# A gated recurrence and a two-layer MLP on one core: weights as float32 through the input queue, cast on three engines

## The chip, the cores and the metric

The kernel runs on one core of a Trainium2 chip. TensorE (PE) multiplies matrices, VectorE (DVE), ScalarE (ACT) and GpSimd (POOL) do elementwise work, SyncE (SP) issues transfers, and 16 DMA engines carry them. The metric is the device time of one execution in microseconds. Four runs of the kernel before gave a median of 192.86 us (191.88 to 193.99).

## The reference

For each of 4 batches and 8 heads of width 48, a state of 48 x 48 is carried over 768 steps; then an MLP runs over all 3072 tokens.

```python
f = 1.0 / (1.0 + np.exp(-f_logit))
for t in range(S):
    state = f[:, :, t, :, None] * state + np.einsum('bhd,bhe->bhde', k[:, :, t], v[:, :, t])
    y[:, :, t] = np.einsum('bhd,bhde->bhe', q[:, :, t], state)
x = y.transpose(0, 2, 1, 3).reshape(B * S, H * D)     # 3072 x 384
h = x @ w_in                                          # w_in 384 x 2048
return (h * (1.0 / (1.0 + np.exp(-h)))) @ w_out       # w_out 2048 x 384
```

All inputs and the output are float32.

## The kernel before

The sequence is cut into 6 chunks of 128 steps. A **unit** is one chunk of one batch with all eight heads: 24 units, unit u being chunk u // 4 of batch u % 4. Two units form a pair.

One unit's attention part runs so. `f` becomes log-sigmoid on ACT with an exp and a log (`E`, `L`, L467 and L469). PE forms the cumulative sum over steps with a triangular matrix (`cs`, L524) and its totals (L528). ACT takes exp of it with both signs (`ia` L531, `a` L533) and of the totals (`al` L535). GpSimd scales k (`ki`, L537) and casts v to bf16 (`vb`, L539), DVE scales q (`qg`, L541). Both are transposed, by PE (`tq`, L547, copied by DVE at L549) or by a DMA transpose from SP (`qkD`, L551). PE forms the scores (`sc`, L558), DVE masks them (`at`, L562), PE forms y from the state before (L567) and the scores (L571), DVE copies it (`yc`, L575), and PE (`yT`, L579, copied at L581) or a DMA transpose (`xD`, L584) turns it into xT. The state update is `d` on PE (L589), `sd` on DVE (L594, L596) and `su` on GpSimd (L600).

The MLP part takes 128 tokens at a time for the first `single` units (`m1`, four quarters of 12 matmuls, L494; silu L491) and 256, a pair, afterwards (`mi`, eight parts of 6 matmuls, L505; silu L501). The second product of a unit, `mo`, is four quarters of 4 matmuls into one PSUM bank (L515), copied by DVE (`oc`, L518) and stored (`so`, L521), from GpSimd's queue but for the last unit. Silu and exp lie in different ACT tables; each change is a table load (L636).

Weights are float32 in memory and bf16 on chip. Two transfers for w_in (L480) and four for w_out (L485) are issued by GpSimd, which casts on the way; each is issued after the `ki` of a given unit (`w_after`). They share the 16 DMA engines with the loads of f, k, q and v, issued by SP (L460).

No order is written by hand. `make_tasks` lists each step as a task with its engine, an assumed duration, the tasks that it needs and the buffers that it takes (`SLOTS` gives how many of each). `schedule` plays the engines forward: a free engine takes the ready task of lowest due time, and the due time of unit u is `pace` times u plus the task's entry in `rank`. The resulting order on each engine is the program: every engine runs its list in order and waits where an input is late. `idle` finds PE's planned gaps up to 60 us and fills part of them with matmuls on a blank tile (L611).

Of the kernel before, what the change touches and what calls it, by code (L numbers as in the profile page):

```python
# [11 lines left out]
F32 = mybir.dt.float32  # L12
# [10 lines left out]

CFG = dict(
    margin=0.35,
    pace=6.78,
    turned=13,
    y_turned=12,
    dma_rate=195.0,
    w_rate=365.0,  # L30
    w_pieces=[2, 4],
    turn_cost=1.5,
    store_sp=23,
    single=4,
    w_after=(0, 2, 3, 3, 3, 4),
    idle_from=1.2,
    idle_to=60.0,
    idle_gap=0.2,
    idle_fill=0.75,
    hold_exp=0.96,  # L40
    hold_silu=1.31,
    keep_exp=68.72,
    keep_silu=92.03,
    rank=dict(ld=-78.39, E=-35.35, cs=-132.35, ia=-65.9, ki=-165.82, vb=71.85, qg=68.24, tq=-123.51,
              qkc=153.77, sc=-147.76, at=-58.0, y=-49.6, yc=-96.71, yT=-207.05, xc=32.16, d=4.54, sd=-70.93,
              su=-186.8, mi=-108.12, si=7.69, mo=2.91, mstep=2.51, oc=91.95, so=-14.34, wi=-116.82, wo=-9.75),
)

SLOTS = dict(f=6, k=6, q=6, v=6, e=2, lf=3, ia=2, qk=5, vb=6, qkT=4, atm=3, yb=3, xT=4, hT=4, sd=2, al=6, o=4,
             st0=1, st1=1, st2=1, st3=1, mlp=3, sc=1, tq=1, cs=1, yd=1)  # L50

LAT = {"PE": 0.25, "ACT": 0.14, "DVE": 0.14, "POOL": 0.08, "SP": 0.0}
TABLE = 1.29
DEPTH = 2.1
LOAD, TURN, WEIGHT, STORE = (1.2, 0.75, 0.015), (0.9, 0.1, 0.021), (2.2, 1.3, 0.2), (1.6, 1.2, 0.14)
DMA = dict(f=LOAD, k=LOAD, q=LOAD, v=LOAD, qkD=TURN, xD=TURN, wi=WEIGHT, wo=WEIGHT, so=STORE)


# [10 lines left out]


def make_tasks(cfg):
    T, tasks, pace, R, X = {}, [], cfg["pace"], cfg["rank"], {}

    def add(name, *a, **k):
        t = Task(name, *a, **k)
        T[name] = t
        tasks.append(t)
        return t
# [4 lines left out]
    def inst(key, cls):  # L83
        if key not in I:
            I[key] = Inst(key, cls)
        return I[key]

    base = lambda u: pace * u
    for P in range(PAIRS):
        u0 = 2 * P  # L90
        for n, x in enumerate("fkqv"):
            inst((x, P), x)
        groups = [(u0,), (u0 + 1,)] if P < 2 else [(u0, u0 + 1)]
        for us in groups:
            for n, x in enumerate("fkqv"):
                add((x, us), "SP", 0.3 * len(us), base(us[0]) + R['ld'] + n * 0.1, acq=[I[x, P]], load=kb(192 * len(us)))
    load_of = lambda x, u: T[x, (u,)] if u < 4 else T[x, (u - u % 2, u - u % 2 + 1)]

    for P in range(PAIRS):
        us_list = [(2 * P,), (2 * P + 1,)] if P < 2 else [(2 * P, 2 * P + 1)]  # L100
        for us in us_list:
            n = len(us)
            ph = us[0] // 2 - 1 if us[0] >= 4 else 0
            e = add(("E", us), "ACT", 0.067 + 0.32 * n, base(us[0]) + R['E'], deps=[T["f", us]], acq=[inst(("e", us), "e")],
                    use=[I["f", P]], mode="exp", phase=ph)
            add(("L", us), "ACT", 0.067 + 0.32 * n, base(us[0]) + R['E'] + 0.1, deps=[e], acq=[inst(("lf", P), "lf")],
                use=[I["e", us]], mode="exp", phase=ph)
    log_of = lambda u: T["L", (u,)] if u < 4 else T["L", (u - u % 2, u - u % 2 + 1)]

    for u in range(UNITS):  # L110
        c, b, P, B = u // BATCHES, u % BATCHES, u // 2, base(u)
        last, ph = c == CHUNKS - 1, u // 2
        dmat = u >= cfg["turned"]
        for key in ("cs", "ia", "qk", "vb", "qkT", "atm", "yb", "sc", "al"):
            inst((key, u), key)
# [32 lines left out]
            add(("su", u), "POOL", 1.02, B + R["su"], deps=[sd, al], acq=[I["st", u]], use=[I["sd", u], I["al", u]])  # L148

    NI, NO = cfg["w_pieces"]  # L150
    w_mb, after = 3.145728e3 / cfg["w_rate"], cfg["w_after"]
    w_dep = lambda i: [T["ki", after[i]]] if after[i] >= 0 else []
    for n in range(NI):
        add(("wi", n), "POOL", 0.8, R["wi"] + n, deps=w_dep(n), load=w_mb / NI)
    for n in range(NO):
        add(("wo", n), "POOL", 0.8, R["wo"] + n, deps=w_dep(NI + n), load=w_mb / NO)

    for P in range(PAIRS):
        B = base(2 * P + 1)
        if 2 * P < cfg["single"]:  # L160
            for u in (2 * P, 2 * P + 1):
                for j in range(4):
                    h, B1 = inst(("h1", u, j), "mlp"), base(u) + 2 * j * R["mstep"]
                    m1 = add(("m1", u, j), "PE", 0.68, B1 + R["mi"], deps=[X[u], T["wi", j * NI // 4]], acq=[h], use=[I["xT", P]])
                    add(("s1", u, j), "ACT", 0.504, B1 + R["si"], deps=[m1], acq=[I["hT", P]], use=[h], mode="silu")
        else:
            for j in range(NTILES // 2):
                h = inst(("h", P, j), "mlp")
                mi = add(("mi", P, j), "PE", 0.655, B + R["mi"] + j * R["mstep"],
                         deps=[X[2 * P], X[2 * P + 1], T["wi", j * NI // 8]], acq=[h], use=[I["xT", P]])  # L170
                add(("si", P, j), "ACT", 0.504, B + R["si"] + j * R["mstep"], deps=[mi], acq=[I["hT", P]], use=[h], mode="silu")
        for i in range(2):
            u = 2 * P + i
            o = inst(("o", u), "mlp")
            for m in range(4):
                mo = add(("mo", u, m), "PE", 0.655, B + R["mo"] + (4 * i + m) * R["mstep"],
                         deps=([T["s1", u, m]] if u < cfg["single"] else [T["si", P, 2 * m], T["si", P, 2 * m + 1]])
                         + [T["wo", m * NO // 4]] + ([T["mo", u, m - 1]] if m else []),
                         acq=[o], use=[I["hT", P]])
            oc = add(("oc", u), "DVE", 0.47, B + R["oc"] + 4 * i, deps=[mo], acq=[inst(("ob", u), "o")], use=[o])  # L180
            late = u >= cfg["store_sp"]
            add(("so", u), "SP" if late else "POOL", 0.36 if late else 0.6, B + R["so"] + 4 * i, deps=[oc], use=[I["ob", u]],
                load=0.45)
    return tasks, T

# [1 line left out]
def schedule(tasks, slots, cfg, margin=0.0, fixed=None, dur=None):  # L187
# [62 lines left out]
    def dma_to(upto):  # L250
        nonlocal dma_t
        while dma_t < upto - EPS:
            h, s, rate, nxt = heads()
            step = min(upto, nxt if nxt is not None else upto) - dma_t
            dma_t += step
            for k, v, r in (("hw", h, rate[0]), ("sw", s, rate[1])):
                if v:
                    v[1] -= r * step
                    if v[1] <= EPS:
                        q[k].pop(0)  # L260
                        if q[k] and q[k][0][4] != v[4] and k == "hw":
                            q[k][0][1] += cfg["turn_cost"]
                        heapq.heappush(pend, (dma_t + v[3], v[0].idx))
                        heapq.heappush(events, dma_t + v[3])
# [8 lines left out]
    def pick(e, cand):  # L273
        key = lambda t: (t.prio, t.idx)
        if e != "ACT":
            return min(cand, key=key)
        best = {m: min((t for t in cand if t.mode == m), key=key, default=None) for m in ("exp", "silu")}
        mine, other = best[st["mode"]], best["silu" if st["mode"] == "exp" else "exp"]
        if other is None:
            return mine  # L280
        if mine is None:
# [109 lines left out]
def kernel(  # L391
# [27 lines left out]
        xT=([128, KT, 2 * C], BF16), hT=([128, NT, 2 * C], BF16), sd=([C, NP, 2 * D], F32), al=([C, NP], F32),  # L419
        o=([C, d_model], F32), mlp=([128, 512], F32), sc=([C, 2, NP, C], F32), tq=([128, 1024], BF16),  # L420
        cs=([C, 512], F32), yd=([C, HD], F32),
        **{f"st{b}": ([C, NP, 2 * D], BF16) for b in range(B)},
    )
    in_psum = {"mlp", "sc", "tq", "cs", "yd"}
# [46 lines left out]
    def emit(t):  # L471
# [5 lines left out]
        if kind == "wi":  # L477
            w = d_ff // NI
            n = rest[0] * w
            return nc.gpsimd.dma_start(out=w_in_sb[rest[0]], in_=w_in_src[:, :, n:n + w])  # L480
        if kind == "wo":
            m, w = rest[0], NT // NO
            src = moe_w_out[m * w * 128:(m + 1) * w * 128].rearrange("(m p r) d -> p m r d", p=128, r=4)
            dst = w_out_sb[m].rearrange("p (m r) d -> p m r d", r=4)
            return nc.gpsimd.dma_start(out=dst[:, 0] if w == 4 else dst, in_=src[:, 0] if w == 4 else src)  # L485
        if kind in ("m1", "s1"):
            u, j = rest
            P, i = divmod(u, 2)
# [21 lines left out]
        P, i = divmod(u, 2)  # L510
        last = c == CHUNKS - 1
        if kind == "mo":
            o = at("o", u)[:, 0:d_model]
            for n in range(4 * rest[1], 4 * rest[1] + 4):
                nc.tensor.matmul(o, at("hT", P)[:, n, i * C:(i + 1) * C], w_rows(n),  # L515
                                 start=(n == 0), stop=(n == NT - 1))
        elif kind == "oc":
            nc.vector.tensor_copy(at("ob", u), at("o", u)[:, 0:d_model])  # L518
        elif kind == "so":
            r0 = b * S + c * C  # L520
            (nc.sync if t.eng == "SP" else nc.gpsimd).dma_start(out=out[r0:r0 + C, :], in_=at("ob", u))  # L521
# [91 lines left out]
    with tc.manual_schedule():  # L613
# [11 lines left out]
        make_identity(nc, ident)  # L625
        for b in range(B):
            nc.vector.memset(buf[f"st{b}", 0], 0.0)
        acts = [t for t in tasks if t.eng == "ACT"]
        after = {a.idx: b.mode for a, b in zip(acts, acts[1:]) if b.mode != a.mode}
        for t in tasks:  # L630
            while idles and idles[0][0] <= t.start:
# [35 lines left out]
```

## Time and profile before

| | |
|---|---|
| Median of four runs | 192.86 us |
| The profiled execution | 193.99 us, span 191.9 us |
| PE busy | 180.1 us (94%), 15.6 of it on blank matmuls |
| ACT busy | 128.1 us (67%), 26.9 of it in 21 table loads |
| DVE, POOL busy | 92.8 us (48%), 72.7 us (38%) |
| HBM read, written | 25.17 MB, 4.72 MB |
| Last matmul ends | 188.50 us into the span |

Times are of one profiled execution on the core. A group's line gives engine, operation, output and inputs with shapes and count, then busy time and mean duration of one in ns, then the idle time before the group and what ended it. The 40 slices divide the span equally, in tenths busy. Matmuls overlap one another, so the sum of their busy times is more than the time in which they advance.

### The profile page before, as it was taken

How to read it: one execution, taken by the hardware profiler on the slowest of the kernel's cores; microseconds unless marked ns; L12 is line 12 of the kernel's file. 1: busy time of each engine (PE TensorE's matmuls, PEld its weight loads, DVE VectorE, ACT ScalarE, POOL GpSimd, SP SyncE). 2: the span in 40 equal slices, each digit the busy share in tenths (PEclk: the TensorE clock that was granted, in tenths of full speed). 3: DMA queues.
4: the chain of work that ended last, by engine and by line, in shares of the span. 5: the costliest groups of instructions: out<-in, count | busy, mean ns of one | idle time of the engine just before them, and what ended most of it. 6: DMA issues, size and time to landing. Idle time of an engine off the chain costs nothing.

```text
span 191.9 us, 4919 instructions
## 1 busy us (share of the span) xinstructions
PE 180.1 (94%) x2028; PEld 143.8 (75%) x2028; DVE 92.8 (48%) x179; ACT 128.1 (67%) x214; POOL 72.7 (38%) x125
## 2 busy tenths in 40 slices
PE   5989878959999999999999999999999999999992
PEld 4978767945668988778878668878886786877851
DVE  4266247112787547678553764672426455611121
ACT  4424998865048798988896975796795785543600
POOL 2423628003197054372191583194017554101110
PEclk9999999996999999999999999999999999999999
DMA  6999999999999999999529569683995884321112
GB/s 119 183 183 193 219 143 222 209 181 225 221 231 255 223 214 240 197 220 223 112 57 200 130 134 223 137 153 100 224 199 125 168 169 99 106 44 41 41 44 83
DMA packets 118822, 31.12 MB, mean 162 GB/s; under 512 B 116288, under 2 KB 116416, under 8 KB 118800
## 3 DMA queue, kind: packets, MB, share of 16 engines
q1 hardware_dynamic: 115952, 23.14, 62.8%
q0 software_dynamic: 2848, 7.67, 16.0%
q8 instruction: 16, 0.26, 0.6%
q14 instruction: 6, 0.05, 0.1%
HBM read 25.17 MB, written 4.72 MB: 156 GB/s over the span
## 4 chain that ended last, share of the span: by engine, by line
PE 72%; SPq 12%; DMA 9%; ACT 3%; issue 1%; DVE 1%; DVEq 0%
PE mlp L515 31%; PE mlp L505 27%; SPq L460 12%; DMA q<-in_q_dram 9%; PE sc L558 3%; PE yd L571 2%; PE yd L567 2%; PE cs L524 2%; PE tq L547 2%; PE yd L589 2%; ACT L636 1%; ACT hT L501 1%; PE tq L579 1%; PE cs L528 1%; ACT ia L531 0%
## 5 line engine op out<-in xcount | busy, mean ns | idle before, releaser
L515 PE MATMUL mlp<-w_out,hT 128*128 128x384 bf16 x384 | 71.9, 330 | 0.0
L501 ACT ACTIVATE hT<-mlp 128x512 bf16<-128x512 f32 x80 | 47.1, 597 | 24.9 <-PE mlp L505 22.2
L505 PE MATMUL mlp<-xT,w_in 128*128 128x256 bf16 x480 | 58.2, 273 | 0.2 <-ACT hT L501 0.2
L505 PEld LDWEIGHTS <-w_in 128*128 128x128 bf16 x480 | 51.3, 114 | 3.0 <-issue 0.5
L515 PEld LDWEIGHTS <-hT 128*128 128x128 bf16 x384 | 35.3, 98 | 20.1 <-issue 1.2
L562 DVE TENSOR_TENSOR atm<-sc,triu 128x512 bf16<-128x512 f32 x48 | 30.9, 685 | 18.0 <-PE sc L558 18.0
L537 POOL TENSOR_TENSOR qk<-k,ia 128x384 bf16<-128x384 f32 x24 | 23.9, 996 | 30.6 <-ACT al L535 24.5
L636 ACT ACT_TABLE_LOAD x21 | 26.9, 1283 | 0.4
L539 POOL CAST vb<-v 128x384 bf16<-128x384 f32 x24 | 11.8, 502 | 37.9 <-DMA v<-in_v_dram 26.8
L521 POOL DMA_DIRECT2D out_dram<-o x23 | 13.1, 570 | 32.7 <-DVE o L518 29.6
L600 POOL TENSOR_TENSOR st<-sd,al 48x192 bf16<-48x192 f32 x40 | 20.1, 502 | 12.7 <-DVE sd L594 8.0
L518 DVE COPY o<-mlp 128x384 f32<-128x384 f32 x24 | 13.3, 555 | 22.2 <-PE mlp L515 22.1
L531 ACT ACTIVATE ia<-cs 128x384 f32<-128x384 f32 x24 | 11.7, 486 | 16.7 <-PE cs L528 13.3
L541 DVE TENSOR_TENSOR qk<-q,cs 128x384 bf16<-128x384 f32 x24 | 13.2, 551 | 19.7 <-ACT cs L533 12.6
L575 DVE CAST yb<-yd 128x384 bf16<-128x384 f32 x24 | 13.3, 554 | 16.3 <-PE yd L571 16.3
L611 PE MATMUL mlp<-blank 128*128 128x128 bf16 x184 | 15.6, 249 | 1.0 <-DVE blank L616 1.0
L467 ACT ACTIVATE e<-f 128x768 f32<-128x768 f32 (+1 forms) x14 | 10.5, 747 | 8.6 <-DMA f<-in_f_logit_dram 8.6
L611 PEld LDWEIGHTS <-blank 128*128 128x128 bf16 x184 | 13.4, 114 | 1.4 <-DVE blank L616 1.0
L549 DVE COPY qkT<-tq 128x1024 bf16<-128x1024 bf16 x13 | 8.9, 688 | 6.9 <-PE tq L547 6.9
L494 PE MATMUL mlp<-xT,w_in 128*128 128x128 bf16 x192 | 11.6, 219 | 0.4 <-DVE xT L581 0.2
L594 DVE TENSOR_TENSOR sd<-yd,st 128x384 f32<-128x384 f32 x16 | 8.8, 553 | 6.3 <-PE yd L589 5.9
L533 ACT ACTIVATE cs<-cs 128x384 f32<-128x384 f32 x24 | 11.4, 477 | 0.6
(38 smaller groups left out, 147.0 us busy)
## 6 DMA issues: line engine op xcount, KB each, us to landing
out_dram<-o POOLq DMA_DIRECT2D x23, 192.0 KB, 3.5
f<-in_f_logit_dram SPq DMA_DIRECT2D x10, 384.0 KB, 5.7
k<-in_k_dram SPq DMA_DIRECT2D x10, 384.0 KB, 6.1
q<-in_q_dram SPq DMA_DIRECT2D x10, 384.0 KB, 5.6
v<-in_v_dram SPq DMA_DIRECT2D x10, 384.0 KB, 6.1
w_in<-in_moe_w_in_dram POOLq DMA_DIRECT2D x2, 768.0 KB, 8.1
w_out<-in_moe_w_out_dram POOLq DMA_DIRECT2D x4, 384.0 KB, 8.1
f<-in_f_logit_dram SPq DMA_DIRECT2D x4, 192.0 KB, 3.7
```

Source lines behind the costliest of these rows:

```text
L460: nc.sync.dma_start(out=dst, in_=SRC[x].rearrange("b h s d -> s (b h) d")[c * C:(c + 1) * C, b * H:(b + n) * H])
L501: return nc.scalar.activation(at("hT", P)[:, 2 * j:2 * j + 2, :], h, AF.Silu)
L505: nc.tensor.matmul(h[:, i, :], w_tile(kk, n), at("xT", P)[:, kk, :], start=(kk == 0), stop=(kk == KT - 1))
L515: nc.tensor.matmul(o, at("hT", P)[:, n, i * C:(i + 1) * C], w_rows(n), start=(n == 0), stop=(n == NT - 1))
L518: nc.vector.tensor_copy(at("ob", u), at("o", u)[:, 0:d_model])
L537: nc.gpsimd.tensor_mul(at("qk", u)[:, 1, :, 0:D], at("k", P)[:, i], at("ia", u))
L541: nc.vector.tensor_mul(at("qk", u)[:, 0, :, 0:D], at("q", P)[:, i], at("cs", u)[:, 0:HD].rearrange("p (h d) -> p h d", d=D))
L562: nc.vector.tensor_mul(at("atm", u)[:, r], at("sc", u)[:, r], triu[:, None, :].to_broadcast([C, NP, C]))
L575: nc.vector.tensor_copy(at("yb", u), at("y", u))
L600: nc.gpsimd.tensor_mul(at("st", u)[lo:lo + D, :, r * D:(r + 1) * D], at("sd", u)[lo:lo + D, :, r * D:(r + 1) * D], at("al", u)[lo:lo + D, ...
L611: nc.tensor.matmul(buf["mlp", bank][:, 0:C], blank, blank, start=True, stop=True, skip_group_check=True)
L636: nc.scalar.preload_act_table_set(SETS[after[t.idx]])
```

## The change

- The weights are read as float32 by SP's queue, in the same list as f, k, q and v: w_in in four pieces of 512 columns into four staging tiles (`ws`), w_out in four pieces into two (`wt`). Their places among the loads of the first units are fixed by `w_at`.
- Eight tasks (`ci`, `co`) cast a piece each to bf16: five on GpSimd, two on DVE, one on ACT. The products wait for the cast.
- The second product of units 0 and 1 is formed in two halves in two PSUM banks, copied and added by DVE.
- Units 4 and 5 too run their MLP 128 tokens at a time; one more unit's queries and keys go by DMA transpose and three units' y fewer; stores from unit 11 on go by SP's queue.
- f, k, q, v have 5 buffers in place of 6; xT, hT and o have 3 in place of 4.
- `pace` and all of `rank` have other values, the loads of the first eight units have fixed places, and ACT may take a task that needs no table. The order on every engine is therefore another.

```diff
-    pace=6.78,
-    turned=13,
-    y_turned=12,
+    pace=2.02,
+    turned=12,
+    y_turned=15,
...
-    w_pieces=[2, 4],
+    w_pieces=(4, 4),
...
-    store_sp=23,
-    single=4,
-    w_after=(0, 2, 3, 3, 3, 4),
+    store_sp=11,
+    single=6,
+    w_at=(3.4, 2.93, 3.01, 3.21, 3.55, 3.06, 4.0, 3.68),
+    cast=('POOL', 'POOL', 'POOL', 'DVE', 'POOL', 'DVE', 'ACT', 'POOL'),
+    halves=2,
...
-SLOTS = dict(f=6, k=6, q=6, v=6, e=2, lf=3, ia=2, qk=5, vb=6, qkT=4, atm=3, yb=3, xT=4, hT=4, sd=2, al=6, o=4,
+SLOTS = dict(f=5, k=5, q=5, v=5, ws=4, wt=2, e=2, lf=3, ia=2, qk=5, vb=6, qkT=4, atm=3, yb=3, xT=3, hT=3, sd=2, al=6, o=3,
...
-                add((x, us), "SP", 0.3 * len(us), base(us[0]) + R['ld'] + n * 0.1, acq=[I[x, P]], load=kb(192 * len(us)))
+                add((x, us), "SP", 0.3 * len(us), base(us[0]) + R['ld'] + n * 0.1 if us[0] >= 8 else us[0] + 0.25 * len(us) * n - 1000.0, acq=[I[x, P]], load=kb(192 * len(us)))
...
-        add(("wi", n), "POOL", 0.8, R["wi"] + n, deps=w_dep(n), load=w_mb / NI)
+        add(("wi", n), "SP", 0.45, cfg["w_at"][n] - 1000.0, acq=[inst(("ws", n), "ws")], load=24 / NI * ROW[8 // NI] * 2)
...
+    for j in range(4):
+        for m, (x, w, N) in enumerate((("wi", "ws", NI), ("wo", "wt", NO))):
+            e = cfg["cast"][4 * m + j]
+            add(("ci" if x == "wi" else "co", j), e, CAST[e], cfg["rank0"]["cw"] + 1.0 * j + 4.0 * m, deps=[T[x, j * N // 4]], use=[I[w, j * N // 4]])
...
-            return nc.gpsimd.dma_start(out=w_in_sb[rest[0]], in_=w_in_src[:, :, n:n + w])
+            return nc.sync.dma_start(out=at("ws", rest[0]), in_=w_in_src[:, :, n:n + w])
...
+            if t.eng == "ACT":
+                return nc.scalar.copy(dst, src)
+            return (nc.vector if t.eng == "DVE" else nc.gpsimd).tensor_copy(dst, src)
...
-                                 start=(n == 0), stop=(n == NT - 1))
+                                 start=(n % (NT // 2 if half else NT) == 0), stop=(n == NT - 1 or half and n == NT // 2 - 1))
+        elif kind == "oa":
+            nc.vector.tensor_copy(at("ob", u), at("o", u, 0)[:, 0:d_model])
         elif kind == "oc":
-            nc.vector.tensor_copy(at("ob", u), at("o", u)[:, 0:d_model])
+            if u < CFG["halves"]:
+                nc.vector.tensor_add(at("ob", u), at("o", u, 1)[:, 0:d_model], at("ob", u))
+            else:
+                nc.vector.tensor_copy(at("ob", u), at("o", u, 0)[:, 0:d_model])
```

## The prediction

> **What bounds the kernel now.** I began with the page's table of 40 slices, for where TensorE really works.
>
> ```profile
> PE   5989878959999999999999999999999999999992
> ...
> PEclk9999999996999999999999999999999999999999
> DMA  6999999999999999999529569683995884321112
> ```
>
> From the tenth slice on PE is full; before that it is not, while the DMA engines are full. The chain that ended last, in order of time, says what the head waits for:
>
> ```profile
> 21.28 3.37 SPq L460
> ...
> 24.69 17.87 DMA q<-in_q_dram
> ...
> 42.65 0.57 DVE qk L541
> ...
> 43.66 0.47 PE tq L547 x8
> ```
>
> The q load of units 4 and 5 is issued at 24.69 and lands at 42.56, because weights share the engines. The issue table shows the queue of those weights:
>
> ```profile
> w_in<-in_moe_w_in_dram POOLq DMA_DIRECT2D x2, 768.0 KB, 8.1
> w_out<-in_moe_w_out_dram POOLq DMA_DIRECT2D x4, 384.0 KB, 8.1
> ```
>
> Last, the groups by form, for durations, and a table by stage:
>
> ```profile
> L515 PE MATMUL mlp<-w_out,hT 128*128 128x384 bf16 x384 | 71.9, 330 | 0.0
> L501 ACT ACTIVATE hT<-mlp 128x512 bf16<-128x512 f32 x80 | 47.1, 597 | 24.9 <-PE mlp L505 22.2
> L636 ACT ACT_TABLE_LOAD x21 | 26.9, 1283 | 0.4
> L611 PE MATMUL mlp<-blank 128*128 128x128 bf16 x184 | 15.6, 249 | 1.0 <-DVE blank L616 1.0
> L539 POOL CAST vb<-v 128x384 bf16<-128x384 f32 x24 | 11.8, 502 | 37.9 <-DMA v<-in_v_dram 26.8 <-PE yd L589 8.8 <-issue 1.9
> ```
>
> ```profile
> 40.00:45.00 5.00, 2.97 (x27) 1.89 (x26) 1.37 (x3) 2.87 (x5) 0.93 (x3) 0.97 0.90 181
> 45.00:50.00 5.00, 5.00 (x34) 2.59 (x33) 1.84 (x4) 1.69 (x2) 0.97 (x2) 0.69 1.17 225
> 66.00:74.00 8.00, 7.70 (x92) 6.20 (x90) 4.68 (x10) 7.79 (x15) 3.54 (x5) 1.00 1.11 232
> ```
>
> The columns are PE, PEld, DVE, ACT, POOL busy, clock, DMA share, GB/s. All 184 blank matmuls lie before 31 us, so a busy PE in the head is partly filler. PE busy time overlaps, so I count work by the step between matmuls in the chain: a quarter of a second product (4 matmuls) 0.65 us, an eighth of a pair's first product 0.655, a quarter of a single unit's 0.68, scores 0.33, y 0.20 and 0.17 for its state part, d 0.17, cumulative sum 0.27, query/key transposes 0.45, y transposes 0.17. Over all units: 96 x 0.65 + 80 x 0.655 + 16 x 0.68 + 24 x 0.33 + 24 x 0.20 + 20 x 0.17 + 20 x 0.17 + 6.1 (sums) + 13 x 0.45 + 12 x 0.17 = 159.2 us. By 44.13, where the chain becomes unbroken PE, only 19.4 of that is done (16 single quarters 10.9, two second-product quarters 1.3, attention 7.2). The head has lost 24.7 us. The other 139.8 end at 188.50, so 4.6 are lost in the dense part: 1.55 to the clock (0.31 of 5 us), the rest in small gaps. The tail after 188.50 is 3.4 us, and 2.1 lie outside the 191.9 us span of the profiled execution (193.99).
>
> **Part by part: the DMA.** The weights leave GpSimd's casting queue for SP's. What they cost today follows from the landing of that q load: f of unit 0 lands at 3.8, f of unit 1, four loads on, at 7.6, so 0.96 us for each 192 KB load; the later 384 KB loads are issued 1.85 us apart, with stores between. 16 x 0.96 + 3 x 1.85 + 2.85 = 23.8; the other 18.8 are the six weight transfers, 2.35 us for each eighth of their float32 bytes (768 KB). The new transfer is not in the trace; the same bytes are read, without the cast, in rows of 2 KB and 6 KB. The Trainium skill ("DMA: Bandwidth & Descriptors", the rules for kernel authors) says to issue a cast during DMA from GpSimd, which is against this change; its fit, 2.0 us fixed plus bytes at 436 GB/s, makes 768 KB 1.8 us of movement. Bounds 1.8 and 2.35; I take 2.1, since the 8.1 us landing shows the casting queue never had the engines to itself, and the eight 16.8. The rule alone would keep before's 44; my sum moves the start because the order changes too.
>
> **The order in SP's queue** after the change: 12 loads of units 0 to 2, then w_in 1, f3, w_in 2, w_out 1, w_in 3, k3, w_in 0, q3, w_out 0, w_out 3, v3, f of 4 and 5, w_out 2, k, q, v. Landings: v2 at 3.8 + 11 x 0.96 = 14.4; q3 after five weight pieces and three loads, 14.4 + 10.5 + 2.9 = 27.8; q of 4 and 5 at about 40.5, where it was 42.6.
>
> **Casts.** Eight, of 1536 elements per partition, none shown at that size. ACT: 384 to 768 elements goes 0.52 to 0.84, so 1.5. GpSimd: its 384-element cast takes 0.50, so at most 2.0; with a fixed part like DVE's, 1.5; I take 1.6. DVE: from 0.555 (384) and 0.685 (512, two inputs) at most 1.75; half of that if it runs two elements a cycle; I take 0.9. They are 8 us on GpSimd, 1.8 on DVE and 1.5 on ACT, none of which fills the head. What matters is the waits they add, engines being in order. DVE waits for w_out 1 (21.6) and w_in 3 (23.7), and behind it y's copy of unit 2 and thus its first product wait until 25. GpSimd waits for w_in 0 (26.7) and w_out 0 (29.8), with unit 2's state update and unit 3's v cast behind. ACT waits for w_out 2 (36.8) with unit 4's exponentials behind; what they feed needs k and q of units 4 and 5, landing at 38.6 and 40.5, anyway. SP waits for the two reused w_out staging tiles: it wants to issue w_out 3 near 28 and the cast that frees it ends at 22.5; w_out 2 near 32.5 and 31.4. All are covered by q3; without cover each costs up to 2 us.
>
> **Where PE gets going.** Unit 3's q lands at 27.8; gate on DVE 0.55, then the transposes: 29.1. Ahead of that in PE's order stand seven single quarters (4.75), four cumulative sums 1.1, four transposes 1.8, three scores 1.0, three each of y, d, y transposes 1.6: 10.2 us. From here I walked PE's order against the landings: w_in 0 is cast by 28.4, the first wait past it is w_out 0 at 31.4 against its use at 33, and q of 4 and 5 at 40.5 against its use at 41. I find no wait of over half a us after that. The waits before 29.1 are late together, so shortening one is worth nothing.
>
> **Work.** Single units go from 4 to 6: 8 x 0.68 - 8 x 0.655 = +0.2; one query/key transpose fewer, -0.45; three y transposes more, +0.5: 159.45 in all. The two second products in halves add no matmul and two DVE adds of 0.55 beside an idle DVE; they let w_out 0 and 1 be used before 2 and 3. Two more table loads, 2.6 us on ACT. Stores 11 to 22 move from GpSimd to SP (12 x 0.57 off GpSimd); SP then waits for each o copy with loads and transposes behind it, against a queue that stood waiting 17 us for one store. Buffers f, k, q, v fall from 6 to 5, xT, hT and o from 4 to 3: nothing while loads lead by a pair; one load late is 5.7 us.
>
> **The clock.** Blank matmuls fall from 184 to 112, and I find PE idle for about 1.9 us before w_in 3 and 1.5 before q3. The gap from 40.9 to 43.26, 2.4 us, was followed by a clock of 0.69. The Trainium skill ("TensorE: Matmul & The Clock Gate", Part 1) puts the fall after an idle window of about 3.4 us. By the rule the two gaps cost nothing, by the row up to 1.55. The row decides; I keep 4.6 for all losses of the dense part, as before.
>
> **Sum.** 29.1 + (159.45 - 10.25) + 4.6 = 182.9 for the last matmul against 188.5: 5.6 less. The profiled execution goes from 193.99 to 188.4; it stood 1.13 over the median, so 187.3 us. Weights at 1.8 give 185.8, at 2.35 188.6.
>
> **Rivals.** (1) The clock pays for the missing blanks: twice 5 us at 0.69, plus weights at 2.35: 187.3 + 1.3 + 3.1 = 191.7, no measurable change (a difference under 1% can't be told apart here). For it: 0.69 after only 2.4 us. Against: gaps shorter, in work that partly waits anyway.
>
> (2) ACT becomes the bound between 34 and 74, and the kernel is slower. There it must do 8 table loads 10.2, 4 exp/log pairs 6.7, the cast 1.5, 6 gate sets 6.5 and 20 silus 11.3 = 36.2 us, in four rounds of exp and silu, while PE's work is 40. If each round's silus come 2 us late PE stands still four times: 187.3 + 8 = 195.3. It decides from 1.85 us a round (7.5 in all). For it: ACT 7.79 of 8 us busy in 66 to 74. Against: PE still worked there and waited 0.24.
>
> (3) Gains beyond the sum: weights at 1.8 and the clock never falls, 185.8 - 1.5 = 184.3.
>
> **Numbers.** Forecast 0.52 (185.8 to 189), rival 1 0.18, rival 2 0.17, rival 3 0.13. Faster by over 1%: 0.52 + 0.13 + a little of rival 1 = 0.68; within 1%: 0.15; slower 0.17. The range runs from 184.3 to 192.5, which leaves most of rival 2 out.
>
> **What would show it.** The transposes of unit 3 near 29 us, q of 4 and 5 landing near 40.5, the chain all PE from about 30, clock 1.0 but for one slice, last matmul near 183. Wrong if GpSimd's casts take over 2.5 us, if a landing of weights passes 2.5 us apiece, or if ACT waits appear in the chain after 44.

## The result, and the profile after

The changed kernel took a median of 189.96 us (189.42 to 191.30, 12 runs) where the kernel before, on the same chip, took 192.41 (191.85 to 194.56, 17 runs): ratio 0.9858, 95% interval 0.9824 to 0.9891. Run again on another chip it gave 189.36 us, ratio 0.9912 (0.9875 to 0.9950). It is faster by 0.9 to 1.4%. Scaled to the 192.86 us that the prediction started from, the two results are 190.1 and 191.2 us, where it expected 187.3. The profiled execution took 190.4 us, with a span of 188.6; the prediction's sum for it was 188.4. The two profiles lie 3.6 us apart and the medians only 2.45, since the profiled execution of the kernel before (193.99) was one of its longest: one of the 17 took longer.

The table of 40 slices of the changed kernel:

```profile
PE   5998739999999999979999999999999999999991
...
PEclk9999996999999999999999999999999999999999
DMA  6989999899999999998999499468785765413101
```

PE is full from the seventh slice on instead of the tenth (the 7 in the eighteenth is a wait that comes up below), and the DMA engines are full or nearly so until the 22nd. The one slice of low clock has moved from 45 to 50 us into the head. The issue table has the weights in SP's queue now (KB of each, median us to landing):

```profile
ws<-in_moe_w_in_dram SPq DMA_DIRECT2D x4, 768.0 KB, 8.7
wt<-in_moe_w_out_dram SPq DMA_DIRECT2D x4, 768.0 KB, 7.9
```

The chain that ended last (start, us, what):

```profile
15.42 10.77 DMA ws<-in_moe_w_in_dram
...
26.21 0.97 DVE w_in L520
...
29.91 1.28 PE mlp L529 x12
31.19 0.65 PE tq L588 x8
31.84 1.34 PE mlp L529 x24
...
35.64 1.30 PE mlp L551 x8
...
37.14 1.30 PE mlp L551 x8
...
38.78 1.30 PE mlp L551 x8
...
41.70 1.30 PE mlp L551 x8
...
43.24 0.47 PE tq L588 x8
...
179.62 5.21 PE mlp L551 x32
...
184.91 0.56 DVE o L559
```

The head now waits for w_in 3 and its cast on DVE. Unit 3's transposes stand at 31.19, unit 4's at 43.24, and PE works without a pause between them. The last matmul is done when DVE starts to copy at 184.91, against 188.50 before. PE's longest wait in the head, and the stages (PE, PEld, DVE, ACT, POOL busy, clock, DMA share, GB/s):

```profile
PE mlp L529 <- DVE w_in L520: 2.9, 1, 2.9
```

```profile
25.00:30.00 5.00, 2.77 (x34) 2.77 (x35) 1.78 (x3) 0.97 (x2) 1.81 (x2) 0.81 1.08 367
30.00:35.00 5.00, 5.00 (x80) 4.81 (x78) 3.00 (x5) 2.61 (x5) 4.25 (x5) 0.85 1.04 259
...
40.00:45.00 5.00, 5.00 (x75) 4.28 (x73) 1.80 (x3) 4.51 (x8) 2.82 (x5) 1.00 1.20 229
45.00:50.00 5.00, 5.00 (x54) 3.32 (x53) 3.41 (x7) 4.55 (x8) 1.89 (x4) 1.00 0.94 204
```

The hole of 2 us that stood in 40 to 45 is gone, and the clock of 45 to 50 is full.

In the prediction's own terms the 3.6 us between 188.50 and 184.91 come from four places. The transposes of unit 4 end 0.42 earlier (43.71 against 44.13). By then 22.1 us of work are done instead of 19.4: the 10.2 up to unit 3's transposes, the 11.4 that PE works between 31.84 and 43.24, and unit 4's transposes; that is 2.7. Most of it is six quarters of second products more (the four rows x8 of L551 above are eight quarters), against two quarters of first products fewer. The kernel before had only two such quarters there and then stood:

```profile
39.76 1.46 PE L515 MATMUL mlp<-w_out,hT 128*128 128x384 bf16 x8
43.26 0.32 PE L524 MATMUL cs<-lf,triu 128*128 128x384 bf16 x1 [2.03 <-DVE qk L541]
```

The change adds 0.25 of work. The dense part after that loses 3.8 instead of 4.6. So 0.42 + 2.7 - 0.25 + 0.8 = 3.7, to rounding.

### The profile page after: what moved, and what is told of

It reads as the page before. It is cut to its first block, busy times and chain, and to the rows that moved or that the text cites. A ratio compares the mean times of both kernels' runs of the same rounds, so it can differ in the third digit from the quotient of the medians.

```text
span 188.6 us, 4875 instructions
## 1 busy us (share of the span) xinstructions
PE 176.2 (93%) x2005; PEld 141.4 (75%) x2005; DVE 96.0 (51%) x185; ACT 131.1 (69%) x217; POOL 69.7 (37%) x112
## 4 chain that ended last, share of the span: by engine, by line
PE 78%; SPq 7%; DMA 6%; ACT 5%; issue 1%; DVE 1%; ACTq 0%; DVEq 0%
PE mlp L551 32%; PE mlp L540 24%; PE mlp L529 8%; DMA ws<-in_moe_w_in_dram 6%; SPq L485 6%; PE sc L599 3%; PE yd L612 2%; PE yd L608 2%; PE tq L588 2%; PE cs L565 2%; PE yd L630 2%; ACT L677 2%; SPq L505 2%; PE tq L620 1%; ACT hT L536 1%
## 5 line engine op out<-in xcount | busy, mean ns | idle before, releaser
L551 PE MATMUL mlp<-w_out,hT 128*128 128x384 bf16 x384 | 69.9, 326 | 0.0
L536 ACT ACTIVATE hT<-mlp 128x512 bf16<-128x512 f32 x72 | 41.7, 597 | 17.4 <-PE mlp L540 14.9
L540 PE MATMUL mlp<-xT,w_in 128*128 128x256 bf16 x432 | 51.5, 273 | 1.1 <-ACT hT L536 1.0
L551 PEld LDWEIGHTS <-hT 128*128 128x128 bf16 x384 | 34.8, 97 | 19.5
L540 PEld LDWEIGHTS <-w_in 128*128 128x128 bf16 x432 | 46.3, 114 | 3.2 <-issue 1.3
L529 PE MATMUL mlp<-xT,w_in 128*128 128x128 bf16 x288 | 20.0, 227 | 3.2 <-DVE w_in L520 2.9
L559 DVE COPY o<-mlp 128x384 f32<-128x384 f32 x22 | 12.2, 556 | 18.3 <-PE mlp L551 14.6
L529 PEld LDWEIGHTS <-w_in 128*128 128x128 bf16 x288 | 18.1, 117 | 4.0 <-DVE w_in L520 3.0
L526 ACT ACTIVATE hT<-mlp 128x512 bf16<-128x512 f32 x24 | 13.6, 596 | 7.9 <-PE mlp L529 7.5
L574 ACT ACTIVATE cs<-cs 128x384 f32<-128x384 f32 x24 | 11.4, 477 | 0.6
L652 PE MATMUL mlp<-blank 128*128 128x128 bf16 x112 | 10.8, 269 | 1.0 <-DVE blank L657 1.0
L494 ACT ACTIVATE lf<-e 128x768 bf16<-128x768 f32 (+1 forms) x14 | 10.5, 750 | 0.4
```

The costliest lines, as they stand in the source:

```text
L526: return nc.scalar.activation(at("hT", P)[:, 4 * j:4 * j + 4, i * C:(i + 1) * C], h, AF.Silu)
L529: nc.tensor.matmul(h[:, r, :], w_tile(kk, 4 * j + r), at("xT", P)[:, kk, i * C:(i + 1) * C], start=(kk == 0), stop=(kk == KT - 1))
L536: return nc.scalar.activation(at("hT", P)[:, 2 * j:2 * j + 2, :], h, AF.Silu)
L540: nc.tensor.matmul(h[:, i, :], w_tile(kk, n), at("xT", P)[:, kk, :], start=(kk == 0), stop=(kk == KT - 1))
L559: nc.vector.tensor_copy(at("ob", u), at("o", u, 0)[:, 0:d_model])
```

## The experiments

Three questions were open: whether the input queue or the order gave the gain, why it was 3.6 and not 5.6 us, and whether the second could be mended.

**The hole before w_in 3, filled with blanks.** PE stands for 2.9 us before w_in 3, and in that execution the clock fell to 0.81. Here PE works on blank matmuls in that hole, 42 in place of 2.

```diff
-                warm(*idles.pop(0)[1:])
+                at_, bank_, n_ = idles.pop(0)
+                warm(bank_, 42 if n_ == 2 else n_)
```

> The changed kernel (189.96 us) with 42 blank matmuls in place of 2 in PE's wait for w_in 3, so that PE does not idle from 24.4 to 27.2; nothing else moves. Theory A, that part of the missing gain went to the clock: the granted clock in 25 to 35 us goes from 0.81 and 0.85 to about 1.0, unit 3's transposes end near 31.0 in place of 31.84, and the time falls by 1.0 to 1.6 us to about 188.6. Theory B, that the landings of the weights alone set the head: clock 1.0 but the last matmul within 0.3 us of 184.9, time within 0.5 us of 189.96.

Measured: 189.82 us, ratio 0.9931 (0.9894 to 0.9968). The clock was 1.00 in the profiled execution and the unit 4 transposes came at 42.44, 0.8 earlier than in the changed kernel's first profile, but no gain in time can be told. It is neither A, whose 188.6 us did not come, nor quite B, since the last matmul ended at 183.99. The control below had the same hole without blanks, and its clock stayed at 1.00 too; and q of units 4 and 5 landed at 41.31 here with no transfer moved, so the 0.8 can't be put down to the blanks.

**The weights through GpSimd's casting queue again.** The new order and everything else stay; only the eight weight transfers go from GpSimd, straight into the bf16 tiles, and the eight casts are gone (the `return` at the end of the cut).

```diff
-            return nc.sync.dma_start(out=at("ws", rest[0]), in_=w_in_src[:, :, n:n + w])
+            return nc.gpsimd.dma_start(out=w_in_sb[rest[0]], in_=w_in_src[:, :, n:n + w])
...
-            return nc.sync.dma_start(out=dst[:, 0] if w == 4 else dst, in_=src[:, 0] if w == 4 else src)
+            return nc.gpsimd.dma_start(out=dst[:, 0] if w == 4 else dst, in_=src[:, 0] if w == 4 else src)
...
+            return
```

> The changed kernel's orders on every engine, but the eight weight pieces are again read and cast by GpSimd's queue, issued at the same places of the planned order, straight into the bf16 tiles, and the eight cast instructions are dropped. Theory A, that the order made the gain and the way of the weights costs the DMA engines the same (2.35 us a piece against 2.45 seen): time within 1.2 us of 189.96, with loads and weights landing side by side and not one after the other. Theory D, that the input queue itself made the gain: the time goes back to 192 or above.

Measured: 189.98 us, ratio 0.9924 (0.9887 to 0.9960), unit 4's transposes at 42.91. The casting queue does as well in this order. So the queue and the three casting engines, which give the change its name, are not where the time comes from; it comes from what else the change brings. That this is the order, with the places of the weights among the loads, is what the second products in the head point to; single units, halves, buffers and order were not taken apart. PE waits at the same place, only for another releaser:

```profile
PE mlp L530 <- DMA w_in<-in_moe_w_in_dram: 3.7, 1, 3.7
```

The loads come out otherwise, too: with the weights beside them and not among them, q of units 4 and 5 lands near 39.4, 2.6 us before the changed kernel's, and it is w_in 3 that is late.

**One piece fewer.** w_in 3 isn't transferred; its cast reads w_in 1's tile, so that a quarter of the first product uses other columns.

```diff
+        if kind == "wi" and rest[0] == 3:
+            return
...
-                ... at("ws", n)[:, :, 512 * i:512 * i + 512]
+                ... at("ws", 1 if n == 3 else n)[:, :, 512 * i:512 * i + 512]
```

> The changed kernel without the transfer of w_in 3; its cast reads the tile of w_in 1 in place of it, so a quarter of the first product uses other columns. One 768 KB transfer is gone ahead of k3, w_in 0 and q3. Theory A: q of unit 3 lands 2.1 to 3.2 us earlier, PE does not wait at w_in 3, and the last matmul comes 2 to 3.5 us earlier, time about 187. Theory C: a later wait takes over and the time falls by under 1 us.

Measured: 187.66 us, ratio 0.9805 (0.9769 to 0.9841). This is the one experiment that moved the time below the changed kernel's (0.9912 in the control, 0.9931 and 0.9924 in the two runs beside it; only the first measurement's interval, from 0.9824, touches its own), and it is the one that takes bytes away. Its chain:

```profile
32.35 6.67 DMA q<-in_q_dram
...
40.16 0.47 PE tq L590 x8
```

The q of units 4 and 5 lands at 39.02, and the end moves with it, by 3.1 us against the changed kernel's first profile and by 2.2 to 2.3 against the two other profiles with its list of transfers (blanks, stores).

**The changed kernel as a control**, on another chip.

> The changed kernel itself, as the measure on this chip for the runs beside it: 1.0% to 1.8% under the kernel before.

Measured: 189.36 us, ratio 0.9912. Its chain is not that of the first profile. It goes through a second wait:

```profile
22.05 7.90 DMA q<-in_q_dram
...
30.51 0.56 DVE sd L637
...
31.14 0.51 POOL st L641
...
32.29 1.48 POOL w_out L520
...
33.79 0.45 SPq L510
...
34.76 7.27 DMA q<-in_q_dram
...
42.15 0.56 DVE qk L582
...
43.16 0.47 PE tq L588 x8
```

Read from above: q of unit 3 lands, DVE and GpSimd update unit 2's state, and only then GpSimd casts w_out 0. That cast frees the staging tile for w_out 2, and SP stands before it. Behind it in SP's queue are k and q of units 4 and 5. SP's own waits, and the list of what it issued, say for how long:

```profile
SPq L510 <- DMA wt<-in_moe_w_out_dram: 2.8, 1, 2.8
SPq L510 <- POOL w_out L520: 1.9, 1, 1.9
```

```profile
27.13 1.91 SPq L485 DMA_DIRECT2D f<-in_f_logit_dram  x1
33.79 0.45 SPq L510 DMA_DIRECT2D wt<-in_moe_w_out_dram  x1
```

SP was ready at 29.0 and stood until 33.8. The first 2.8 us of that are for w_out 0 itself, which lands at 31.8; the state update, done at 32.2, holds the cast back by less than half a us. That made two suspects: the late q of unit 3, and the blocked queue.

**w_out 1 behind q of unit 3.** w_out 1 is moved behind q of unit 3 in SP's list, its cast behind the copy of unit 3's transposes, and what hangs on it follows. A first build, w_out1_later, let w_out 3 overwrite w_out 1's staging tile before its cast, so that a quarter of the second product used other weights and the cast waited for w_out 3; it doesn't measure the move.

```diff
+    move(("wo", 1), ("q", (3,)))
+    move(("co", 1), ("qkc", 3))
+    move(("wo", 0), ("wo", 1))
+    move(("v", (3,)), ("wo", 0))
+    move(("wo", 3), ("v", (3,)))
+    move(("co", 3), ("vb", 3))
```

> The changed kernel with w_out 1, which no product needs before 35 us, moved in SP's list from before w_in 3 to behind q of unit 3, and its cast on DVE behind the copy of unit 3's transposes; v of unit 3 moves ahead of w_out 3, and the cast of w_out 3 behind that of v. Theory A, that the head ends with w_in 3, then q of unit 3, and everything after follows one for one: w_in 3 lands near 24 in place of 26.2, q of unit 3 near 27.8 in place of 29.95, unit 3's transposes end near 29, and the time falls by 2.2 to 3 us to about 187.4, the clock staying near 1. Theory C, that a later wait (the loads of units 4 and 5, or ACT between 34 and 74) takes over: the transposes come earlier, the time falls by under 1 us.

Measured: 191.34 us, ratio 1.0002 (0.9964 to 1.0040), with a wait of PE of 2.5 us for that cast. As a test of the move it is inconclusive.

The second build has the same moves, and w_out 3 gets the staging tile that w_in 1 has left.

```diff
+    where[("wt", 3)] = where[("ws", 1)].rearrange("p k n -> p (k n)").rearrange("p (m d) -> p m d", d=d_model)
```

> As in w_out1_later, w_out 1 moves behind q of unit 3 in SP's list and its cast behind the copy of unit 3's transposes on DVE; w_out 3 is now staged in the tile of w_in 1, long free, so that its transfer waits for no cast and nothing of it can overwrite w_out 1. Theory A, the head ends with w_in 3 and q of unit 3 and all after it follows: w_in 3 lands near 24, q of unit 3 near 27.8, unit 3's transposes end near 29, time 2.2 to 3 us under the changed kernel. Theory C, after that the landing of q of units 4 and 5, whose place in the list is unchanged, holds PE: w_in 3 and q of unit 3 earlier as in A, PE waits near 41 for units 4 and 5, and the time falls by only 0.5 to 1.2 us, as with the blank matmuls in the gap (0.8 us of span).

Measured: 189.43 us, ratio 0.9918 (0.9881 to 0.9954), beside 0.9912 for the control on the same chip. q of unit 3 lands at 27.35 instead of 29.95 and its transposes start at 28.1, 2.7 us before the control's 30.8; and the time is the same. The waits of PE say why:

```profile
PE tq L603 <- DVE qk L597: 1.4, 1, 1.4
PE cs L580 <- DVE qk L597: 1.2, 1, 1.2
```

The second line is the wait for q of units 4 and 5, which lands at 41.42. What PE gains at unit 3 it waits for at unit 4.

**The staging tiles of w_out 2 and 3.** Both pieces go to tiles of w_in that are free long before, so that no tile should hold SP. Nothing is moved in the first kernel; the second has the moves above as well, and was meant to leave neither suspect.

```diff
+    for m in (2, 3):
+        where[("wt", m)] = where[("ws", 4 - m)].rearrange("p k n -> p (k n)").rearrange("p (m d) -> p m d", d=d_model)
```

> The changed kernel with the third and fourth pieces of w_out staged in the tiles of w_in 2 and w_in 1, so that the input queue doesn't stand waiting for GpSimd's cast of w_out 0 (SP stood from 29.0 to 33.8 there). Nothing else is moved. Every theory: w_out 2 is issued near 29, the q of units 4 and 5 lands at 39 to 40.5 in place of 42, and unit 3's transposes stay at 31.2 to 31.8. Theory 'the blocked queue is what ended the time': the last matmul ends 1.5 us or more earlier, about 187.6 us. Theory 'the late transposes of unit 3 end it, the queue only once they are early': at most 0.8 us less than the changed kernel, 188.6 to 189.4.

> The same new staging, and in the order list the cast of w_out 1 with its store of unit 2 and what follows it moved behind the first product by q of unit 3, as in w_out1_after_q3. Theory 'two waits in a row, the late q3 and then the queue blocked on staging': unit 3's transposes near 28.4, the q of units 4 and 5 at 39 to 40, PE dense from about 29, last matmul at 182 to 183, time 187.0 to 187.8 and so under both kernels. Rival 'another wait takes over again': last matmul no earlier than 184, time within 0.6 us of the changed kernel.

Measured: restaged 189.43 us, ratio 0.9933 (0.9891 to 0.9975); restaged_reordered 189.27 us, ratio 0.9903 (0.9869 to 0.9937). The 39 to 40.5 expected for q of units 4 and 5 failed in both: it lands at 41.32 and 41.19. SP's list in restaged seems to say that the issue of w_out 2 now lasts 5.11 us:

```profile
28.50 5.11 SPq L512 DMA_DIRECT2D ws<-in_moe_w_out_dram  x1
```

SP's own waits and the chain of the same execution show what is in it:

```profile
SPq L512 <- POOL w_out L522: 4.6, 1, 4.6
```

```profile
31.62 1.48 POOL w_out L522
33.10 0.52 SPq L512
```

The tile was free (the cast of w_in 2 out of it ran from 20.70 to 22.17), but SP still stood until GpSimd's cast of w_out 0 had ended, and the issue proper took 0.52. In restaged_reordered the same item lasts 5.57 us (27.91 to 33.48), of which SP waits 5.2 for GpSimd, here until the cast of v behind that of w_out 0:

```profile
SPq L526 <- POOL vb L596: 5.2, 1, 5.2
```

```profile
32.62 0.46 POOL vb L596
33.09 0.39 SPq L526
...
34.42 6.78 DMA q<-in_q_dram
```

So these two kernels took the tile away as a reason and not the wait: the blocked queue was not removed, and what it costs stays open. Why SP still waits for GpSimd there, these runs don't show. That it stood does cost the DMA engines work: in restaged_reordered their share falls to 0.14 from 33 to 34 us; in the changed kernel it is 0.57 and 0.76 in the two us from 34, which makes some 0.7 us, as an estimate.

**What one piece costs alone.** Two kernels load the eight pieces into eight tiles with nothing beside them, one through the input queue as float32, one through the casting queue to bf16; the rest of the computation is left out, and a small read by DVE marks each landing.

> Only the eight float32 weight pieces, one after the other by SP's queue into eight tiles, and one element of each read by DVE as it lands; all else is left out and the output is zeros. Theory A, a piece costs what it costs in the kernel whatever runs beside it: 2.35 to 2.45 us apart. Theory E, that alone it costs the Trainium skill's price and the loads of 192-byte rows around it make it dearer: 1.8 to 2.0 us apart.

> The same eight pieces alone, read and cast to bf16 by GpSimd's queue. Theory A: 2.35 us apart, as worked out from the landing of q of units 4 and 5 in the kernel before. Theory E: the same bytes read and half of them written, 1.8 to 2.0 us apart. If it is well over 2.4 the cast itself costs the engines time.

Measured, from the first landing to the eighth: 5.45 to 19.41 and 6.35 to 20.23, so 13.96 and 13.88 us for seven pieces, 1.99 and 1.98 each (one execution of each). Both ways cost the same.

**The stores of units 11 to 22 from GpSimd again.**

```diff
-            (nc.sync if t.eng == "SP" else nc.gpsimd).dma_start(out=out[r0:r0 + C, :], in_=at("ob", u))
+            (nc.sync if u == UNITS - 1 else nc.gpsimd).dma_start(out=out[r0:r0 + C, :], in_=at("ob", u))
```

The order is kept; only the queue that issues these stores is another.

> The changed kernel with the stores of units 11 to 22 issued by GpSimd, as before the change. My theory: nothing, within 0.5 us of the changed kernel, since GpSimd isn't what PE waits for there. Rival: GpSimd's state updates come later by the 0.6 us that each store takes it, and PE's wait for them shows: 1 us slower or more.

Measured: 188.90 us (4 runs), ratio 0.9899 (0.9826 to 0.9973). No cost can be seen. This execution's unit 4 transposes fall at 42.35, ahead of the first store that differs, so nothing can be said for a gain either.

**No halves.** All second products whole, and the kernel's own planner makes a new list with that.

```diff
-    halves=2,
+    halves=0,
```

> The changed kernel with the second product of all units whole, none in halves; the kernel's own planner orders it anew, so other tasks move too. Theory 'halves are worth nothing, as in the sum': within 0.5 us of the changed kernel. Rival 'halves fill PE's waits in the head': 0.5 to 2 us slower, with more idle PE time between 20 and 35 us.

Measured: 197.05 us, ratio 1.0285 (1.0206 to 1.0364), far more than either side expected, and not where they looked. The head is no worse (unit 4's transposes at 42.50). The loss sits between 66 and 76:

```profile
66.00:76.00 10.00, 6.63 (x109) 4.88 (x108) 8.89 (x18) 5.95 (x15) 6.87 (x10) 1.00 1.17 250
```

where the changed kernel has PE busy for 10.00 of 10. In its place stands a chain of short steps from engine to engine:

```profile
68.09 1.20 DVE atm L603 x2
69.29 0.60 DVE qkT L590
69.89 0.47 DVE qk L582
...
70.80 0.47 PE tq L588 x8
```

From 67 to 76.4 us PE's list here has no product of the MLP, only attention steps that wait for DVE. So the run measures another order, not the halves; what those are worth stays open.

## Why the prediction was right, and where it was not

**What the runs say of the end.** In every kernel with the changed kernel's list behind unit 4, the last matmuls end a fixed time after unit 4's transposes start (the kernel before, with its own list, stands beside them):

| kernel | q of 4, 5 lands | unit 3's transposes | unit 4's transposes | last matmuls end | difference |
|---|---|---|---|---|---|
| before | 42.56 | 29.2 | 43.66 | 188.42 | 144.76 |
| changed | 42.0 | 31.19 | 43.24 | 184.83 | 141.59 |
| changed, again | 42.03 | 30.8 | 43.16 | 184.70 | 141.54 |
| blanks in the hole | 41.31 | 30.1 | 42.44 | 183.99 | 141.55 |
| casting queue | 39.4 | 31.07 | 42.91 | 184.46 | 141.55 |
| w_out 1 later, first build | 41.6 | 27.1 | 44.38 | 185.92 | 141.54 |
| w_out 1 behind q3 | 41.42 | 28.1 | 42.55 | 184.08 | 141.53 |
| restaged | 41.32 | 30.1 | 42.45 | 183.99 | 141.54 |
| restaged and reordered | 41.19 | 28.0 | 42.32 | 183.86 | 141.54 |
| stores from GpSimd | 41.2 | 30.31 | 42.35 | 183.89 | 141.54 |
| w_in 3 left out | 39.02 | 27.7 | 40.16 | 181.71 | 141.55 |

(Ends here are those of the chain's last group of matmuls; DVE's copy starts some 0.08 later.) Two things release unit 4's transposes. Where PE waits for q, they start 1.13 after it lands. Where PE runs on without a wait, they start 11.8 to 12.05 after unit 3's, the work between. (In the first build of w_out 1 later it is a third, the 2.5 us for the cast.) In the changed kernel the two meet: 42.0 + 1.13 = 43.13, and 31.19 + 12.05 = 43.24. That is why an earlier head alone gave nothing that can be measured: with it, q of units 4 and 5 decides. That q lands between 41.2 and 42.03 in the kernels of the table with all eight pieces in SP's queue, and the two in which no transfer was moved (blanks, stores) have 41.31 and 41.2; so none of the moves shows a gain there. Two things did bring it in: leaving out 768 KB, and the casting queue, with 39.4. But there w_in 3 came late, and the work from unit 3 on decided. The casting queue with w_in 3 earlier was not tried.

**Transposes of unit 3 at 29.1: wrong, 2.7 late (31.84).** The step that failed is the price of a weight piece. The prediction took 2.1 us between bounds of 1.8 and 2.35, for the new queue. f of unit 3 landed at 18.78 where the sum has 14.4 + 2.1 + 0.96 = 17.5; from there to q of unit 3 at 29.95 four pieces and two loads of 0.96 took 11.2, where the sum has 10.3. Spread over the five pieces the 2.15 us make 2.53 each, above the upper bound. In part this is how it is shared out: v of unit 2, which flew beside w_in 1, was already 0.9 late (15.3 and not 14.4). Nor are the pieces even: w_out 1 landed 2.1 after w_in 2, w_in 3 another 3.25 later. In the execution with blanks q of unit 3 landed at 29.25, which makes 2.4. The rest of the 2.7, about 0.6, is the clock: a quarter took 1.28 and the transposes 0.65 where the sum has 0.68 and 0.45.

**q of units 4 and 5 at 40.5: wrong, 1.5 late (0.7 in the best execution of the same transfers).** The same term: over eight pieces 2.1 + 1.5 / 8 = 2.29, near what before's sum gave (2.35). The reason for going below that, that the casting queue never had the engines to itself, falls with the two kernels that load the weights alone: both queues take 2.0 a piece, so the change of queue had nothing to give. The fit in the Trainium skill ("DMA: Bandwidth & Descriptors"), an estimated 1.8, is near the 2.0 that a piece took alone; the row of the kernel before, with the other loads beside it, was the better guide here. That page's rule on casts, which the prediction set against the change, says who has to issue a casting transfer, not that it is faster. With 2.35 the prediction's own sum is 188.6 us. Of the 1.5 that are then left to 190.1, 0.8 are the last matmul (184.9 against 184.15) and 0.7 come from reckoning with one execution of each: before's stood 1.13 over its median, the changed kernel's 0.44.

**SP's wait for w_out 2 ("near 32.5 and 31.4 ... covered by q3"): wrong.** SP was ready at 29.0 and the tile was free at 33.8. The tile is late because w_out 0 landed at 31.8 instead of 29.8, the same price again; GpSimd's cast, behind unit 2's state update, ran from 32.25 to 33.72. It was not covered, and what it costs is not measured, since the restaged kernels still have the wait.

**Casts: right, but for one of DVE's.** GpSimd 1.47 us (1.6), ACT 1.46 (1.5), DVE 0.96 for w_in and 1.18 to 1.20 for w_out (0.9); two of the groups, of the control:

```profile
L520 POOL CAST w_in<-ws 128x1536 bf16<-128x1536 f32 x3 | 4.4, 1468 | 4.1 <-DMA ws<-in_moe_w_in_dram 4.1
L520 DVE CAST w_out<-wt 128x1536 bf16<-128x1536 f32 x1 | 1.2, 1180 | 1.1 <-DMA wt<-in_moe_w_out_dram 1.1
```

**The dense part: near in its sum, not in its parts.** From 31.84 the 149.2 us of work that were left took 153.1, so 3.9 are lost and not 4.6. But 1.55 of the 4.6 were the clock, which costs nothing here: it was 0.50 to 0.54 from 28 to 31 us and 1.00 from 31.84 on, so its loss lies in the head. In its place stands 1.0 in a single wait for silu near 83. That the two sums come near each other is in part luck.

**The clock: neither row nor rule settles it.** The prediction read 2.4 us for the gap that was followed by 0.69; the row of before shown above has 2.03. In the changed kernel PE stood for 2.86 us in one profiled execution and 2.79 in the next; after the first the clock was 0.81 and 0.85, after the second 1.00 throughout. The rule ("TensorE: Matmul & The Clock Gate", Part 1, in the Trainium skill) would have had no fall in either, the row of before one in both. It cost the first execution about 0.1 us at the end: unit 4's transposes fell at 43.24 against 43.16, the second held by q.

**Rival 1** had the right price for the weights, but not its clock: no stage from 35 to 180 us fell below 1.00, and the gain stayed. Its 191.7 lies nearer to the two results, 190.1 and 191.2, than the forecast's 187.3. **Rival 2**, ACT as the bound, came in one place only and small: in 66 to 74 PE was busy for 8.00 of 8, with ACT at 7.34, and the table loads rose to 23 as counted, but from 80 to 85 ACT was busy for 4.95 of 5 and PE for 4.00. PE's only wait for silu is this:

```profile
PE mlp L540 <- ACT hT L536: 1.0, 1, 1.0
```

The list without halves shows that a stage can go wrong in another order, though through DVE and not ACT: there PE worked 6.63 of 10 us, and ACT 5.95. **Rival 3** needed cheaper weights and didn't get them. That halves, buffers and stores cost nothing was borne out for the stores only, as closely as four runs can tell; the buffers weren't tried.

Two of the prediction's signs of being wrong came: a piece that landed 3.25 us after the one before it, and an ACT wait in the chain after 44. So the direction held and the model held, the work left when PE can run on: the last matmul came 2.0 us after the forecast, 2.15 from the price of the weights and 0.6 from the clock, less 0.7 in the dense part. The size did not. The forecast's own band was 185.8 to 189; the result lies in the wider range of 184.3 to 192.5 only because that takes in rival 1. And the step that gives the change its name, another queue for the weights, has no share in the gain that the runs can show.

## What to carry to other kernels

When a load that everything waits for stands behind a fixed volume of transfers, price that volume from the same kernel's own landings: a new queue is no reason for a lower price until a trace shows one. Before a wait is removed, look for the next thing that would release the same instruction; here two of them lay 0.1 us apart, and the repair of one returned nothing measurable. After it is removed, look whether it is gone: a long issue in SP's list was still the wait, as SP's own waits showed. Look for an instruction that everything passes (unit 4's transposes): if the time from it to the end is fixed, one number per run tells what a change did.

## What the runs showed of the hardware that was not expected

- The same 768 KB took 2.0 us alone in either queue (w_in's pieces through SP's queue 2.0 to 2.4, w_out's 1.87 to 1.89) and 2.3 to 2.5 in this kernel, beside loads in rows of 192 bytes that are counted at 0.96; why a single piece of w_in took 3.25 there stays open.
- An issue can hold SP with no wait in the trace: 4.34 us for w_in 0 in the changed kernel (from 17.59) and 10.93 for k of units 4 and 5 in casting_queue (from 18.09), while the DMA engines were full. What ends it, these runs don't show.
- After a pause of PE the granted clock fell to 0.50 for some 3.4 us in most executions and not in all: after waits of 2.0 us (the kernel before, restaged and restaged_reordered), 2.4, 2.5, 2.9 and 3.7, but not after 2.2 and 2.8 in the control.
